# One core, attention with memory beside a gated feed-forward: fewer matmuls, packed score tiles, and transposes taken off the matmul engine

## The chip, the cores and the metric

The kernel runs on one core of one Trainium2 chip. The metric is device time in microseconds (us). Lower is better. A time given for a kernel is the median of its runs. The span is the time from the first to the last instruction of the one run that was profiled.

Five engines matter here. PE does matrix multiplies, DVE elementwise work and 32x32 transposes, ACT exponentials and other functions, and POOL the causal mask. SP only issues DMA transfers. ACT can issue them as well; its issues are called ACTq in the trace, those of SP are called SPq.

## The reference

The input x has 2048 tokens and 512 channels. The output is a per-token mix of two branches that read the same x.

```python
g = sigmoid((x * gate_w).sum(-1, keepdims=True))
out = g * A(x) + (1 - g) * B(x)

def B(x):                       # 512 -> 1792 -> 512
    gate, up = x @ W_gate, x @ W_up
    return (gate * (gate > 0) * up) @ W_down

def A(x):                       # 32 heads of 16 channels, 4 segments of 512 tokens
    q, k, v = x @ wq, x @ wk, x @ wv
    for s in range(4):
        a_dot = softmax(q_s k_s^T / 4 + causal_mask) @ v_s
        a_mem = phi(q_s) @ M / (phi(q_s) @ z + 1e-6)      # phi(t) = t+1 if t>0 else exp(t)
        o_s   = sigmoid(beta) * a_mem + (1 - sigmoid(beta)) * a_dot
        M, z  = M + phi(k_s)^T v_s, z + sum(phi(k_s))
    return concat(o) @ wo
```

## The kernel before

The program is a list of tasks for each engine. A scheduler written in Python runs when the kernel is built. It estimates when each task could start, chooses the order on each engine, and inserts semaphore waits. On the chip every engine then follows its list in order. The products of large weights with x ("weight matmuls" below: Q, K, V, gate, up, down, output) fill the time between the attention tasks.

A score tile has keys on the partitions and queries along the columns. Block `j` of 128 keys is seen only by queries from `128*j` on, so it has 512, 384, 256 or 128 columns. Four heads are computed at once, on four strips of 32 rows of the array. A head has only 16 channels, so K is projected with padded weights `wkp`: pairs of heads go to two padded copies.

```python
# K twice: padded (8 x 4 matmuls of 512 columns a segment), then with tokens on partitions (4 x 4)
for n in range(8):
    ... pe.matmul(A(ep)[:, :], lhsT=wkp[:, kt, n, :], rhs=xT[:, kt, tok0:tok0 + 512], ...)      # L622
for tt in range(TT):                      # not in the last segment
    ... pe.matmul(A(ep)[:, :], lhsT=xT[:, kt, ...128 tokens...], rhs=wk[:, kt, :], ...)         # L642

# scores and exp: one group and one exp for each key block j
for n in range(8):                        # 4 segments x 8 x 4 = 128 groups
    for j in range(4):
        N = 512 - 128 * j
        for jj in range(4):
            ... pe.matmul(PL[:, jj, 0:N], lhsT=kp16[32*jj:32*jj+32, s2, n, 128*j:128*j+128],
                          rhs=qT16[32*jj:32*jj+32, s2, G, 128*j:512], tile_position=(32*jj, 0)) # L771
        act.activation(E[:, e, :, 0:N], PL[:, :, 0:N], Exp, scale=SCALE)                        # L777
        pool.affine_select(E[:, e, :, 0:128], ...)        # causal mask of the diagonal block   # L779

# value product, then turned to tokens-on-partitions by PE
... pe.matmul(A(epv)[32*jj:32*jj+17, 128*j:512], lhsT=vaug[:, s2_, j, h, :], rhs=E[...])        # L722
dve.tensor_copy(pvT[:, r, :], A(epv)[:, :])
for i in range(4):
    pe.transpose(Tm[:, i*128:(i+1)*128], pvT[:, r, i*128:(i+1)*128], ident)                     # L738
... divide by the row sum into adot; adot = adot * gexp + amem;
    pe.transpose of adot into oT (L834), copied by DVE
# ... the feed-forward: DVE does both max(gate, 0) and the product with up                       # L812, L813

# start: one DMA queue, SP, in this order
wk, wq, x chunk 0, wv, gate column, beta, wg, wu, x chunks 1-3, wo, wd     # 4 transposed pieces a chunk
```

`PL` is the one score buffer. It holds four banks of 512 columns, so scores and exp alternate strictly. `A(ep)` is one of four accumulator banks. All of this is cut.

The softmax here doesn't subtract the row's maximum and nothing guards it: scores larger than these inputs give would overflow.

## Time and profile before

| | before |
|---|---|
| device time | 347.67 us (3 runs, 347.4 to 349.05) |
| span in the profile | 346.7 us |
| PE / DVE / ACT busy | 318.3 / 251.4 / 180.5 us |
| weight matmuls | 1040 |
| score groups, exps | 128, 128 |
| PE transposes | 192 |

The lines below are from the profile page: busy time of each engine (share of the span), then the busy share in 40 equal slices in tenths (9 is 90% or more), the granted PE clock in tenths of full speed, then the shares of the chain of waits that ended last, and the group of the exps (count, busy us and mean ns, idle time before them and what ended it).

```profile
span 346.7 us, 6188 instructions
PE 318.3 (92%) x2560; PEld 132.7 (38%) x2560; DVE 251.4 (73%) x560; ACT 180.5 (52%) x165; POOL 91.4 (26%) x141
...
PE   0995899999999999999989889999898999999996
...
PEclk9999699999999999999999999999999999999999
...
PE 74%; DVE 14%; SPq 9%; issue 1%; DMA 1%; ACT 0%; DVEq 0%
...
L777 ACT ACTIVATE E<-psL 128x2048 bf16<-128x2048 f32 (+3 forms) x128 | 158.2, 1236 | 108.5 <-PE psL L771 108.3
```

PE bounds this kernel: it is busy in nearly every slice and is most of the chain. Three slices differ: the first, with no work, the fourth, half full, and the fifth, with a lower clock. The timeline of PE shows them. Its columns are start, length, engine, line, operation, tiles, count, and in brackets the idle time before with what ended it.

```profile
8.86 6.50 PE L609 MATMUL psA<-xT,wq 128*128 128x512 bf16 x16 [8.86 <-DVE wkp L547]
...
35.91 1.84 PE L581 MATMUL psA<-gwc,xT 128*128 128x1 bf16 x64 [5.37 <-DMA xT<-in_A_x_dram]
...
38.42 3.62 PE L642 MATMUL psA<-wk,xT 128*128 128x512 bf16 x8
41.84 1.99 PE L609 MATMUL psA<-xT,wq 128*128 128x512 bf16 x8
```

Nothing runs for 8.86 us. At 30 us PE stands for 5.37 us, because the tiny gate product (one column) needs all of x and PE works in order. After both pauses the clock is half for a while: eight K matmuls need 3.62 us at 38.42, eight Q matmuls 1.99 us at 41.84.

Between those, the same timeline shows what single steps cost. These are four PE transposes, four weight matmuls, four more, and a score group of 128 columns.

```profile
157.00 0.40 PE L738 MATMUL psA<-ident,pvT 128*128 128x128 bf16 x4
157.23 1.03 PE L609 MATMUL psA<-xT,wq 128*128 128x512 bf16 x4
158.10 1.03 PE L801 MATMUL psA<-xT,wg 128*128 128x512 bf16 x4
159.06 0.23 PE L771 MATMUL psL<-qT,kp 32*128 32x128 bf16 x4
```

Lengths overlap, because a matmul's end lies after the start of the next. The time something costs PE is the step from its start to the next start. Four weight matmuls cost 158.10 - 157.23 = 0.87 us (about 216 ns each) and four transposes 0.23 us.

Summed over the whole trace in this way (each matmul counted until the next one starts or it ends itself, whichever comes first; this is my own working from the trace's times), the 318.3 us of PE are 243.6 us of weight matmuls, 32.0 of scores, 20.8 of value products, 12.5 of transposes and 9.4 of memory and gate products. The rest of the span is idle: 8.9 us at the start, 16.4 in between and 3.1 at the end. Of the 16.4 us, 5.4 are the wait for x above. The groups of instructions put 2.9 us to the transposes at L834, which wait for DVE's last combination, 2.7 us to weight matmuls that wait for an accumulator which DVE's memory reads (L682) still hold, and 3.4 us to scores that wait for an exp.

Entering a score group or value product from a weight matmul costs PE something too. The last weight matmul before one takes 312 or 309 ns to the next start instead of 216. There are 120 such places in this trace, which makes 11.6 us; a transpose after a weight matmul adds next to nothing of this kind.

### The profile page before, as it was taken

What the parts mean: (1) busy time and instruction counts of PE and PEld (TensorE: products, weight loads), DVE (VectorE), ACT (ScalarE), POOL (GpSimd) and SP (SyncE); (2) the same over time, 40 slices, a digit from 0 to 9 for tenths busy, and PEclk for the clock granted to TensorE, in tenths of its full rate; (3) what the DMA queues carried; (4) which work ended last, traced back from release to release, by engine and by line L of the source; (5) the groups of instructions that cost most, each with busy time, mean ns of one, the idle gap of its engine ahead of it and who ended that gap; (6) DMA issues with size and microseconds to landing.
All of it is one profiled execution on the core that took longest, in us unless ns stands there. A gap on an engine that the chain in (4) does not pass through costs nothing.

```text
span 346.7 us, 6188 instructions
## 1 busy us (share of the span) xinstructions
PE 318.3 (92%) x2560; PEld 132.7 (38%) x2560; DVE 251.4 (73%) x560; ACT 180.5 (52%) x165; POOL 91.4 (26%) x141
## 2 busy tenths in 40 slices
PE   0995899999999999999989889999898999999996
PEld 0331443434444444444443334433433334444442
DVE  7685399999998642699899896337988843679621
ACT  1566476566675555577654665555555555450000
POOL 8021023222224222222232232222332222220000
PEclk9999699999999999999999999999999999999999
DMA  7795440000000000000000000000000000000000
GB/s 183 258 306 94 139 145 2 0 3 3 0 3 2 0 17 30 17 0 3 2 0 2 0 2 0 32 16 17 0 2 0 2 15 32 16 2 0 2 30 31
DMA packets 16699, 12.19 MB, mean 35 GB/s; under 512 B 9760, under 2 KB 15648, under 8 KB 16672
## 3 DMA queue, kind: packets, MB, share of 16 engines
q1 hardware_dynamic: 16672, 11.81, 11.8%
q8 instruction: 20, 0.33, 0.4%
q14 instruction: 7, 0.06, 0.1%
HBM read 7.61 MB, written 2.10 MB: 28 GB/s over the span
## 4 chain that ended last, share of the span: by engine, by line
PE 74%; DVE 14%; SPq 9%; issue 1%; DMA 1%; ACT 0%; DVEq 0%
PE psA L857 14%; PE psA L806 13%; PE psA L801 12%; SPq L503 8%; PE psL L771 7%; PE psA L722 5%; PE psA L622 5%; PE psA L849 4%; PE psA L642 3%; PE psA L609 3%; DVE adot L824 3%; PE psA L631 3%; PE psA L738 3%; DVE amem L682 2%; DVE hT L813 2%
## 5 line engine op out<-in xcount | busy, mean ns | idle before, releaser
L777 ACT ACTIVATE E<-psL 128x2048 bf16<-128x2048 f32 (+3 forms) x128 | 158.2, 1236 | 108.5 <-PE psL L771 108.3
L779 POOL TENSOR_SCALAR_AFFINE_SELECT E<-E 128x512 bf16<-128x512 bf16 x128 | 83.9, 655 | 219.6 <-ACT E L777 219.6
L806 PE MATMUL psA<-xT,wu 128*128 128x512 bf16 x224 | 57.8, 380 | 1.6 <-DVE amem L682 1.3
L801 PE MATMUL psA<-xT,wg 128*128 128x512 bf16 x224 | 57.7, 380 | 0.9 <-DVE amem L682 0.8
L857 PE MATMUL psA<-wd,hT 128*128 128x512 bf16 x224 | 53.1, 380 | 0.8 <-DVE hT L813 0.8
L813 DVE TENSOR_TENSOR hT<-psA,rl 128x512 bf16<-128x512 f32 x56 | 38.5, 688 | 9.7 <-PE psA L806 8.6
L812 DVE TENSOR_SCALAR rl<-psA 128x512 bf16<-128x512 f32 x56 | 38.4, 686 | 7.1 <-PE psA L801 6.4
L771 PE MATMUL psL<-qT,kp 32*128 32x256 bf16 (+3 forms) x512 | 40.4, 305 | 3.4 <-ACT E L777 3.4
L861 DVE SCALAR_TENSOR_TENSOR osb<-psA,omg_all,zero 128x512 bf16<-128x512 f32 x16 | 12.0, 751 | 35.7 <-PE psA L857 34.4
L771 PEld LDWEIGHTS psL<-qT,kp 32*128 32x128 bf16 x512 | 12.9, 91 | 54.5 <-issue 27.1
L622 PE MATMUL psA<-xT,wkp 128*128 128x512 bf16 x128 | 31.0, 380 | 0.9 <-DVE amem L682 0.6
L857 PEld LDWEIGHTS psA<-wd,hT 128*128 128x128 bf16 x224 | 20.5, 98 | 24.8 <-issue 1.6
L732 DVE CAST pvT<-psA 128x512 bf16<-128x512 f32 x32 | 22.0, 689 | 10.4 <-PE psA L722 10.0
L801 PEld LDWEIGHTS psA<-xT,wg 128*128 128x128 bf16 x224 | 19.7, 98 | 24.9 <-DVE amem L682 2.3
L806 PEld LDWEIGHTS psA<-xT,wu 128*128 128x128 bf16 x224 | 18.9, 98 | 23.4 <-DVE amem L682 2.1
L609 PE MATMUL psA<-xT,wq 128*128 128x512 bf16 x64 | 18.3, 435 | 8.9 <-DVE wkp L547 8.9
L625 DVE CAST kp<-psA 128x512 bf16<-128x512 f32 x32 | 21.9, 686 | 5.0 <-PE psA L622 4.8
L722 PE MATMUL psA<-E,vaug 128*17 128x256 bf16 (+3 forms) x512 | 23.1, 300 | 0.2 <-DVE hT L813 0.2
L682 DVE SCALAR_TENSOR_TENSOR amem<-psA,gexp,ndrec 128x128 bf16<-128x128 f32 x48 | 16.4, 342 | 0.7
L849 PE MATMUL psA<-wo,oT 128*128 128x512 bf16 x64 | 16.5, 380 | 0.1
L743 DVE RECIPROCAL rden<-psA 128x16 f32<-128x16 bf16 x32 | 8.0, 250 | 11.6 <-PE psA L738 11.6
L622 PEld LDWEIGHTS psA<-xT,wkp 128*128 128x128 bf16 x128 | 11.1, 98 | 13.5 <-issue 0.9
(65 smaller groups left out, 260.3 us busy)
## 6 DMA issues: line engine op xcount, KB each, us to landing
out_dram<-osb SPq DMA_DIRECT2D x16, 128.0 KB
wg<-in_B_W_gate_dram SPq DMA_DIRECT2D x1, 1792.0 KB
wu<-in_B_W_up_dram SPq DMA_DIRECT2D x1, 1792.0 KB
wd<-in_B_W_down_dram SPq DMA_DIRECT2D x1, 1792.0 KB
wk<-in_A_wk_dram SPq DMA_DIRECT2D x1, 512.0 KB
wq<-in_A_wq_dram SPq DMA_DIRECT2D x1, 512.0 KB
wv<-in_A_wv_dram SPq DMA_DIRECT2D x1, 512.0 KB
wo<-in_A_wo_dram SPq DMA_DIRECT2D x8, 64.0 KB
```

The lines of the kernel that those rows point to most:

```text
L609: ins = pe.matmul(A(ep)[:, :], lhsT=wq[:, kt, G * 128:(G + 1) * 128], rhs=xT[:, kt, tok0:tok0 + 512], start=(kt == 0), stop=(kt == KT - 1))
L622: ins = pe.matmul(A(ep)[:, :], lhsT=wkp[:, kt, n, :], rhs=xT[:, kt, tok0:tok0 + 512], start=(kt == 0), stop=(kt == KT - 1))
L722: ins = pe.matmul(A(epv)[32 * jj:32 * jj + 17, 128 * j:512], lhsT=vaug[:, s2_, j, h, :], rhs=E[:, es[j], jj, 0:N], start=(j == 0), stop=(j ...
L771: ins = pe.matmul(PL[:, jj, 0:N], lhsT=kp16[32 * jj:32 * jj + 32, s2, n, 128 * j:128 * j + 128], rhs=qT16[32 * jj:32 * jj + 32, s2, G, 128 ...
L777: act_t.append(Tk("act", lambda ac, e=e, N=N: ac.activation(E[:, e, :, 0:N], PL[:, :, 0:N], ACT.Exp, scale=SCALE), reads=[f"bankL{q4}" for ...
L779: pool_t.append(Tk("pool", lambda pl, e=e: pl.affine_select(out=E[:, e, :, 0:128], in_=E[:, e, :, 0:128], compare_op=ALU.is_ge, fill=0.0, ...
L801: ins = pe.matmul(A(ep)[:, :], lhsT=wg[:, kt, f * 128:(f + 1) * 128], rhs=xT[:, kt, tok0:tok0 + 512], start=(kt == 0), stop=(kt == KT - 1))
L806: ins = pe.matmul(A(ep)[:, :], lhsT=wu[:, kt, f * 128:(f + 1) * 128], rhs=xT[:, kt, tok0:tok0 + 512], start=(kt == 0), stop=(kt == KT - 1))
L812: dve_t.append(Tk("dve", lambda dv, ep=epg, r=r: dv.tensor_scalar(rl[:, r, :], A(ep)[:, :], 0.0, None, ALU.max), writes=[f"rl{r}"], dur=c_ ...
L813: dve_t.append(Tk("dve", lambda dv, ep=epu, r=r, f=f: dv.tensor_tensor(hT[:, f, :], A(ep)[:, :], rl[:, r, :], ALU.mult), reads=[f"rl{r}"], ...
L849: ins = pe.matmul(A(ep)[:, :], lhsT=oT[:, G, i * 128:(i + 1) * 128], rhs=wo[:, G, :], start=(G == 0), stop=False)
L857: ins = pe.matmul(A(ep)[:, :], lhsT=hT[:, f, i * 128:(i + 1) * 128], rhs=wd[:, f, :], start=False, stop=(f == NF - 1))
```

## The change

The intent is to take work off PE, which bounds, and put some of it on engines with time left.

- **One K projection.** K is projected once, without padding. DVE writes two masked copies in place of the padded heads. The token-major copy for the memory comes from a DMA transpose of `ek`. PE does 928 weight matmuls in place of 1040.
- **Packed score tiles.** Blocks of 384+128 and 256+256 columns share a full tile of 512. There are 80 groups and 80 exps of one shape, in place of 128 of four shapes. The columns are the same in all.
- **No PE transposes.** DVE transposes the value product by 32x32 blocks, twice. The memory's result is turned by DMA. 192 PE transposes disappear.
- **A new scheduler.** It may also place the feed-forward's ReLU and the last scaling on ACT or on DVE.
- **A new start.** All weights are issued by ACT and x by SP, both from the first moment, and twelve dummy matmuls warm up PE.

The diff is very long, since the file is nearly rewritten. This is its core; cuts are marked with `...`.

```diff
 # start
-    all loads queued on "sp": wk, wq, x0, wv, gate, beta, wg, wu, x1..x3, wo, wd
+    def wload(name, dst, src, nbytes):
+        loads.append(dma("act", lambda e: e.dma_start(dst, src), nbytes, ...))
+    ... wq, wk, gate column, beta, wv, wg0, wu0, wg1, wu1, wo, wd
+    xl = [dma("sp", ... e.dma_start_transpose(V.xT[:, kt, c*512:(c+1)*512], A_x[...])) ...]
+    def f_warm(e):
+        for i in range(12):
+            e.matmul(PL[:, 0, :], lhsT=V.rl[:, 0, 0:128], rhs=V.rl[:, 0, :], start=True, stop=True)
 # K
-    for n in range(8): ... matmul(lhsT=wkp[:, kt, n, :], rhs=xT...)        # padded
-    for tt in range(TT): ... matmul(lhsT=xT..., rhs=wk[:, kt, :])           # token-major
+    ep = pj(V.wk, G, "k", "wk")                                             # 4 projections, once
+    dve.tensor_copy(V.kT[:, G, :], A(ep)[:, :])
+    for p in range(2):
+        dve.tensor_scalar(V.kp[:, ks, :], V.kT[:, G, :], V.pm[:, p:p+1], None, mult)   # L538, mask
+    ... phi into V.ek; sp.dma_start_transpose(V.phik[...], V.ek[:, G, :])
 # scores
-    for j in range(4): group of 512 - 128*j columns, exp of the same width
+    eA[0] = quad(f"{G}A0", [(n0, 0, 0, 512)])
+    eB[0] = quad(f"{G}B0", [(n0, 1, 0, 384), (n0, 3, 384, 128)])
+    flush()                                       # value products of the pair of heads before
+    eC = quad(f"{G}C", [(n0, 2, 0, 256), (n1, 2, 256, 256)])
+    ... A1, B1 for n1
+    act.activation(V.E[:, e, :, :], PL[:, :, :], Exp, scale=SCALE)          # L620, always 4 x 512
 # after the value product
-    dve.tensor_copy(pvT, A(epv)); pe.transpose x4; ... pe.transpose of adot; dve copies
+    dve.transpose(V.Tn[:, p, :], A(ep)[:, :])                               # L645
+    ... scale by the row sum and the gate in the transposed layout
+    dve.transpose(V.oTt[:, :], V.adT[:, :])                                 # L657
+    dve.tensor_tensor(V.oT[:, os_, :], V.oTt, V.amemT[:, G, :], add)        # amemT: DMA transpose
 # feed-forward: one operation, two possible engines
-    dve.tensor_scalar(rl, A(ep), 0.0, None, max)
+    Op([("act", ... activation(V.rl[:, r, :], A(ep)[:, :], Relu)), ("dve", ... tensor_scalar(... max))])
 # queues of PE, by priority
+    sc.queue(0, Q["patt"])     # scores and value products in ONE strict order
+    sc.queue(1, Q["pmu"]); sc.queue(1, Q["pnd"]); sc.queue(2, Q["pproj"]); sc.queue(3, Q["pout"]); sc.queue(4, Q["pffn"])
```

## The prediction

> **What bounds it now.** Engine table: PE busy 318.3 of 346.7 us (92%), DVE 251.4 (73%), ACT 180.5 (52%). PE is 74% of the chain of waits. PE's 28 us idle, by the groups and waits views: 8.9 us before the first Q matmul, 5.4 us for the last x chunks at 30 to 36 us, about 3 at the end, the rest small stalls. The window table shows a granted clock of 0.62 at 35 to 44 us after that stall; the first 16 Q matmuls run at a 430 ns pitch (timeline) against 216 later. The Trainium skill, "TensorE: Matmul & The Clock Gate" (Part 1), says that the array runs at half rate until about 3.4 us of activity and again after an idle window; the trace agrees both times. Together they cost about 7 us.
>
> **PE work, costed by the timeline's start-to-start times.**
> - 512-column weight matmuls: 1040 to 928, since one K projection (64) replaces a padded (128) and a token-major one (48). At 216 ns: minus 24 us.
> - Score matmuls: same columns, but 80 groups of 512 columns replace 128 groups of 512, 384, 256 and 128. A group costs its columns plus about 0.2 us of entering and leaving: 44 us to 35, minus 9.
> - PE transposes (128+64, about 0.23 us per four) go: minus 11 to 12.
> - Value matmuls, memory update and read: about minus 2.
> Sum: 309 us of full-clock work to about 264. All of it is on the critical path, since PE bounds.
>
> **Other engines (estimates from before's durations).** Exp: 128 instructions, 158 us, become 80 of 1.88 us, 150; with phi, 25 ReLUs and 10 final scalings ACT reaches about 190. DVE loses evictions, 25 ReLUs and chains of small memory operations; it gains 48 transposes of 512 columns (taken as 0.69 us, like its other PSUM reads; the Trainium skill, "VectorE: DVE Perf Modes" (The three transpose paths), has them as 32x32 blocks only, which suits this layout; no run here shows one yet) and 32 masks of 0.29 us. About 208 us, 72% of the new span. Neither becomes the bound. The score/exp loop needs about 80 x 2.6 = 210 us, under PE. DMA transposes for keys and memory should hide inside a segment.
>
> **Start.** Warm-up matmuls should remove most of the 3.5 us of half-rate Q. x transposes now go out on SP from the start, weights on ACT. Before, transposes queued behind the big weights held SP for 4.9 and 5.2 us; now they only share the engines. I expect first Q at 8 to 10 us, and a wait of 2 to 6 us for x chunks around 20 to 32. Danger: ACT issues 6 MB or more of weights before its first activation; if these issues are held likewise, the tiny exp of beta is late, DVE sits behind it in order, PE runs out of accumulators, and up to 10 us are lost.
>
> **Time.** 264 work + 9 start + 3 end + 4 x wait + 2 residual half clock + 8 small stalls = 290 us. Range 278 to 304.
>
> **What would show it right.** 928 weight matmuls at 216 ns; PE busy 265 to 280 including warm-up; score groups about 35 us; 80 exps at 1.88 us; PSUM transposes near 0.69; the chain mostly PE; PE idle about 25 us, mostly at the start; no second half-clock slice, or a short one.
>
> **What would make it wrong.** DVE transposes much slower than 0.69 us, PE waiting for accumulators (above 304). DMA transposes landing several us late, so that memory matmuls, in order on PE, stall each segment. ACT held at the start. Packed score groups have two pieces, which may cost more than I read. On the low side: stalls almost gone, 275 to 280.

## The result, and the profile after

| | before | after |
|---|---|---|
| device time | 347.83 us (4 runs) | 295.57 us (4 runs, 295.05 to 296.37) |
| ratio, 95% interval | | 0.8491, 0.8468 to 0.8513 |
| span in the profile | 346.7 | 293.3 |
| PE busy | 318.3 | 269.9 |
| first Q matmul starts at | 8.9 us | 17.8 us |

A ratio is the mean time of one kernel's fast runs over the mean time of the other's fast runs of the same rounds. It is therefore not quite the ratio of the medians quoted. The result is correct, as are those of all experiments below.

The same lines of the page, for the kernel after:

```profile
span 293.3 us, 5236 instructions
PE 269.9 (92%) x2136; PEld 115.0 (39%) x2172; DVE 198.7 (68%) x391; ACT 184.2 (63%) x142; POOL 93.4 (32%) x150
...
PE   7059989799999999999999999999999999999895
...
PEclk9658979999999999999999999999999999999999
...
PE 85%; DVE 6%; DMA 4%; issue 2%; SPq 1%; ACT 0%; DVEq 0%; ACTq 0%
```

PE still bounds. It is busy from the ninth slice on, and hardly at all in the second, where "before" was at work. The busy share is 92% both times, and yet 53 us are gone: a share alone says nothing of the amount of work.

These lines are the timeline of all engines at the start, in the kernel after.

```profile
0.80 34.50 SPq L437 DMA_TRANSPOSE xT<-in_A_x_dram  x16
1.25 5.30 PE L468 MATMUL psL<-rl 128*128 128x512 bf16 x12 [1.25 <-DVE rl L460]
...
10.17 5.88 ACTq L412 DMA_DIRECT2D wo<-in_A_wo_dram  x1
16.08 2.81 ACTq L412 DMA_DIRECT2D wd<-in_B_W_down_dram  x1
...
17.81 1.87 PE L522 MATMUL psA<-xT,wq 128*128 128x512 bf16 x4 [11.26 <-DMA xT<-in_A_x_dram]
...
20.21 0.23 ACT L472 ACTIVATE eb<-braw 128x32 f32<-128x32 bf16 x1
21.18 1.91 PE L522 MATMUL psA<-xT,wq 128*128 128x512 bf16 x4
...
24.16 1.03 PE L522 MATMUL psA<-xT,wq 128*128 128x512 bf16 x4
```

The warm-up ends at 6.55 us. Then PE stands for 11.26 us until a piece of x lands. The first Q matmuls run at half clock all the same (four in 1.91 us at 21.18; 1.03 at 24.16). ACT's issues of `wo` and `wd` are held for 5.88 and 2.81 us, so its first small exponential comes only at 20.21 us.

The costs of the new operations are in the groups of instructions by shape (count, then busy us and mean ns).

```profile
L620 ACT ACTIVATE E<-psL 128x2048 bf16<-128x2048 f32 x80 | 150.1, 1876 | 44.3 <-PE psL L615 43.8
...
L645 DVE STREAM_TRANSPOSE Tn<-psA 128x512 f32<-128x512 f32 x32 | 21.5, 698 | 17.6 <-PE psA L640 17.4
...
L657 DVE STREAM_TRANSPOSE oTt<-adT 128x512 bf16<-128x512 bf16 x12 | 8.4, 703 | 0.1
```

Next come the same start-to-start sums as before, in us. One correction was needed. The trace of "after" has 2136 matmul records but all 2172 records of weight loads (PEld, one for each matmul). The missing ones are weight matmuls, and without the correction they look like idle time. Where a gap before a weight matmul has one load more than matmuls, I put a matmul back, 216 ns before the next one. That restores 31 of 36 in "after", 46 of 46 in e9 and 31 of 35 in e5; the last few would move about 1 us from idle to weight matmuls. "before" misses none.

The third column is experiment e9 below (the old work under the new scheduler and with a good start), the fourth e5 (the new kernel with a good start).

| | before | after | e9 | e5 |
|---|---|---|---|---|
| span | 346.7 | 293.3 | 328.1 | 281.6 |
| weight matmuls | 243.6 | 212.4 | 239.2 | 210.3 |
| of it, added by half clock | 4.6 | 4.4 | 1.4 | 1.6 |
| scores | 32.0 | 26.4 | 31.8 | 26.4 |
| value products | 20.8 | 19.9 | 21.0 | 19.7 |
| PE transposes | 12.5 | 0 | 12.0 | 0 |
| memory, gate | 9.4 | 9.4 | 9.7 | 9.4 |
| warm-up | 0 | 5.3 | 4.7 | 4.7 |
| idle before the first weight matmul | 8.9 | 12.5 | 4.3 | 4.0 |
| other idle in between | 16.4 | 3.9 | 2.0 | 4.2 |
| end | 3.1 | 3.3 | 3.2 | 2.9 |
| entries from weight matmuls to scores or value products | 120 | 77 | 122 | 78 |

### The profile page after: what moved, and what is told of

Read it like the earlier page. It is cut to its first block, busy times and chain, and to the rows that moved or that the text cites. A ratio compares the mean times of both kernels' runs of the same rounds, so it can differ in the third digit from the quotient of the medians.

```text
span 293.3 us, 5236 instructions
## 1 busy us (share of the span) xinstructions
PE 269.9 (92%) x2136; PEld 115.0 (39%) x2172; DVE 198.7 (68%) x391; ACT 184.2 (63%) x142; POOL 93.4 (32%) x150
## 4 chain that ended last, share of the span: by engine, by line
PE 85%; DVE 6%; DMA 4%; issue 2%; SPq 1%; ACT 0%; DVEq 0%; ACTq 0%
PE psA L685 32%; PE psA L716 17%; PE psA L522 10%; PE psL L615 8%; PE psA L640 6%; PE psA L708 5%; DMA xT<-in_A_x_dram 4%; PE psA L520 4%; SPq L437 1%; DVE vaug L546 1%; DVE kp L538 1%; PE psA L561 1%; PE psA L590 1%; DVE gexpT L494 1%; DVE qT L529 1%
## 5 line engine op out<-in xcount | busy, mean ns | idle before, releaser
L620 ACT ACTIVATE E<-psL 128x2048 bf16<-128x2048 f32 x80 | 150.1, 1876 | 44.3 <-PE psL L615 43.8
L645 DVE STREAM_TRANSPOSE Tn<-psA 128x512 f32<-128x512 f32 x32 | 21.5, 698 | 17.6 <-PE psA L640 17.4
L615 PE MATMUL psL<-qT,kp 32*128 32x384 bf16 (+3 forms) x512 | 31.7, 301 | 0.9 <-ACT E L620 0.8
L522 PE MATMUL psA<-xT,wq 128*128 128x512 bf16 x58 | 18.1, 432 | 11.8 <-DMA xT<-in_A_x_dram 11.3
L693 ACT ACTIVATE rl<-psA 128x512 bf16<-128x512 f32 x25 | 14.9, 596 | 16.8 <-PE psA L685 16.8
L529 DVE CAST qT<-psA 128x512 bf16<-128x512 f32 x16 | 11.0, 688 | 19.4 <-PE psA L522 19.3
L694 DVE TENSOR_SCALAR rl<-psA 128x512 bf16<-128x512 f32 x31 | 21.1, 682 | 4.1 <-PE psA L685 3.6
L640 PE MATMUL psA<-E,vaug 128*17 128x256 bf16 (+3 forms) x512 | 21.1, 300 | 0.0
L522 PE MATMUL psA<-xT,wk 128*128 128x512 bf16 x62 | 18.6, 418 | 0.3 <-issue 0.2
L721 ACT ACTIVATE osb<-psA,omg 128x512 bf16<-128x512 f32 x10 | 6.9, 687 | 17.3 <-PE psA L716 17.3
L520 PE MATMUL psA<-wv,xT 128*128 128x512 bf16 x61 | 15.0, 380 | 0.3 <-issue 0.2
L640 PEld LDWEIGHTS psA<-E,vaug 128*17 128x17 bf16 x512 | 10.5, 90 | 11.2 <-issue 4.2
## 6 DMA issues: line engine op xcount, KB each, us to landing
wg<-in_B_W_gate_dram ACTq DMA_DIRECT2D x2, 896.0 KB, 14.1
```

The costliest lines, as they stand in the source:

```text
L520: ins = e.matmul(A(ep)[:, :], lhsT=V.xT[:, kt, tok + col * 128:tok + (col + 1) * 128], rhs=w[:, kt, :], start=(kt == 0), stop=(kt == KT - 1))
L522: ins = e.matmul(A(ep)[:, :], lhsT=w[:, kt, col * 128:(col + 1) * 128], rhs=V.xT[:, kt, tok:tok + 512], start=(kt == 0), stop=(kt == KT - 1))
L615: ins = q.matmul(PL[:, jj, o:o + w], lhsT=V.kp[32 * jj:32 * jj + 32, kslot(s, n), 128 * j:128 * j + 128], rhs=V.qT[32 * jj:32 * jj + 32, q ...
L620: acts.append(act(lambda a, e=e: a.activation(V.E[:, e, :, :], PL[:, :, :], ACT.Exp, scale=SCALE), t_act(2048), reads=[f"bankL{b}" for b i ...
L640: ins = q.matmul(A(ep)[32 * jj:32 * jj + 17, c:512], lhsT=V.vaug[:, s % 2, j, 8 * G + 2 * jj + p, :], rhs=V.E[:, e, jj, o:o + w], start=(j ...
L645: ds.append(dve(lambda e, p=p, ep=eps[p]: e.transpose(V.Tn[:, p, :], A(ep)[:, :]), t_dve(512), writes=[f"Tn{p}"], name=f"tr{s}_{G}_{p}", e ...
```

## The experiments

The theory from here on: the three parts that take work off PE are worth what their PE time says, about 45 us together, and the new start loses some 10 us of it. The rivals: the gain comes from the scheduler or from the relief of DVE, or the parts are worth something else than their PE time. Twelve kernels were run in three sets (e1 to e4, e5 to e8, e9 to e12); kernels of one set share the runs of "before" (347.8, 348.41 and 348.47 us in the three sets). "After" was run in a set of its own, so a difference to it of less than about 1 us says nothing.

| run | what it is | us | ratio to before | 95% |
|---|---|---|---|---|
| after | the change | 295.57 | 0.8491 | 0.8468 to 0.8513 |
| e1 | after, old K projections | 323.32 | 0.9283 | 0.9247 to 0.9318 |
| e2 | after, scores not packed | 326.35 | 0.9382 | 0.9354 to 0.9411 |
| e3 | after, PE transposes | 323.19 | 0.9303 | 0.9268 to 0.9339 |
| e4 | after, all three undone | 365.53 | 1.0511 | 1.0478 to 1.0544 |
| e5 | after, other start | 283.23 | 0.8114 | 0.8069 to 0.8159 |
| e6 | after, PE's attention queue split | 301.84 | 0.8637 | 0.8597 to 0.8678 |
| e7 | e6, scores not packed | 326.09 | 0.9348 | 0.9299 to 0.9398 |
| e8 | e6, PE transposes | 311.89 | 0.8927 | 0.8881 to 0.8972 |
| e9 | all three undone, queue split, other start | 330.50 | 0.9482 | 0.9442 to 0.9521 |
| e10 | after, no work moved to ACT | 299.20 | 0.8577 | 0.8543 to 0.8612 |
| e11 | e5 without warm-up | 283.04 | 0.8116 | 0.8092 to 0.8140 |
| e12 | e5, longer warm-up, gate copies on ACT and DVE | 282.19 | 0.8088 | 0.8064 to 0.8112 |

### e1: K projected twice again

```diff
-            ep = pj(V.wk, G, "k", "wk")                  # then DVE masks into two copies
+            for p in range(2):
+                ep = pj(V.wkp, 2 * G + p, "k", "wkp")    # padded weights, straight to kp
+        for G in range(4 if s < NSEG - 1 else 0):
+            ep = pj(V.wk, G, "kt", "wk", True)           # token-major, no DMA transpose
```

The padded weights need space, so `hT` has 19 slots instead of 20.

> The changed kernel with its single K projection undone: zero-padded K weights (128 matmuls) plus a token-major K projection (48) in place of 64, no masks and no DMA transposes of the key features; one hidden-layer buffer slot fewer (19 of 20) for room. Theory P (PE is full, so its arithmetic is the time): 112 more matmuls at 0.216 us = 24 us, 318 to 323 us, PE busy about 294. Rival S (the gain came from the new scheduler filling holes, and extra PE work would be hidden in part): under 312. Rival D (DVE load is what mattered): DVE gains about 6 us of evictions net, so 300 to 305.

It took 323.32 us, 27.7 more than "after". 112 matmuls of 216 ns are 24.2 us. PE's busy time on the page rose from 269.9 to 293.9 us, which is 24.0. The rest includes a stall of 2.75 us at 20 us into the run. The time is 0.3 us over the expected range. The part is worth its arithmetic, to within a few us.

### e2: scores not packed

```diff
-            pes.append(pe(fq, ...)); acts.append(act(... E[:, e, :, :] <- PL[:, :, :] ...))
+            for pt in parts:                              # each part its own group and exp
+                o, w = pt[2], pt[3]
+                pes.append(pe(lambda q, pt=pt: fq(q, (pt,)), ...))
+                acts.append(act(... V.E[:, e, :, o:o + w] <- PL[:, :, o:o + w] ...))
```

> The changed kernel with its score tiles unpacked: each piece of 512, 384, 256 and 128 columns is again its own group with its own exp (128 instead of 80), same buffers otherwise. Theory P: 48 more entries and exits of row-tiled groups at about 0.2 to 0.27 us, 305 to 309 us; exp goes from 150 to about 158 us of ACT. Rival S: hidden, 296 to 300. A second rival, that the score/exp loop itself bounds: each of the 48 extra round trips costs 0.5 us or more, over 318.

It took 326.35 us, 31 more. PE's work grew by 14 us (scores 33.7 us instead of 26.4; weight matmuls and value products 6.7 us more, half clock included). The other part is idle time in between, 20.3 us instead of 3.9: PE is at half clock and partly idle from 280 to 307 us. So the arithmetic of 9 us does not explain this run: theory P failed by 17 us, the time is where the second rival had put it (over 318), and e7 was made to find out why.

### e3: PE transposes

```diff
-                e.transpose(V.Tn[:, p, :], A(ep)[:, :])                # DVE
+                e.tensor_copy(V.pvT[:, p, :], A(ep)[:, :])             # DVE
+                q.transpose(A(ep)[...bitcast bf16...], V.pvT[:, p, ...], V.ident)   # PE, x4
...
-            amemT by DMA; e.transpose(V.oTt, V.adT); add
+            adot = adot * gexp + amem; q.transpose(... V.adot ...); e.tensor_copy(V.oT, ...)
```

> The changed kernel with attention output turned by PE again: DVE evicts to bf16, PE transposes 128 + 64 tiles, normalisation token-major, memory term added token-major, no DVE transposes and no DMA transposes of the memory term. DVE time stays about equal. Theory P: PE +12.5 us of transposes plus some entering and leaving: 307 to 311 us. Rival S: hidden in idle PE, 296 to 301. If DMA transposes of the memory term were costing waits in the changed kernel, the result lies lower than P says, 303 to 306.

It took 323.19 us, 27.6 more and 12 above theory P's range, for 14.3 us of transposes. Here too the clock is half near the end, from 284.6 to 305 us, and the idle time in between is 15.8 us. The transposes stood in the one strict queue with the scores. e8 tests that.

### e4: all three undone

This is e1, e2 and e3 together (`hT` 18 slots), with the start of "after".

> All three undone together on the new scheduler, with the changed kernel's start and its choice of ACT or DVE for ReLU and final scaling (hidden-layer slots 18 for room). Theory P: the parts add up, 295.6 + 24 + 11 + 13 = about 341 to 347 us; what is left to the kernel before (347.8) is the scheduler, the ACT/DVE choice and the start together, 1 to 7 us. Rival S: the scheduler is worth 15 us or more, so 320 to 332.

It took 365.53 us, more than "before" and 18.5 above the expected range. The three parts cost 70 us in this form, not 45. The first weight matmul started at 17.4 us, and the idle time in between was 22.3 us. The old work in the new frame, start and queue order included, is worse than the old work in the old frame. e9 separates the start and the queue from the rest.

### e5: another start

```diff
-        loads.append(dma("act", ...))
+        loads.append(dma("act" if name in ("wq", "wk", "braw") else "sp", ...))
-    sc.queue(0, loads)
-    sc.queue(0, xl)
+    sc.queue(0, [w["wq"], w["wk"], w["braw"]])
+    sc.queue(0, xl[0:4] + [w["wv"], w["gw"]] + xl[4:8] + [w["wg0"], w["wu0"]] + xl[8:16]
+                + [w["wg1"], w["wu1"], w["wo"], w["wd"]])
```

The same bytes move, but ACT issues only what the first matmuls need. Everything else stands in one queue with x, in the order in which it is needed.

> The changed kernel with the order of loads alone altered: x chunks, V weights, gate column and the large weights go out on SP in one queue in the order of first use; ACT issues only the Q and K weights and beta. Theory C (in the changed kernel the first x chunk lands at 17.6 us because 6 MB of weights share the DMA engines with it): first Q matmul at 8 to 10 us, half-clock stretch gone or short, 284 to 288 us. Rival T (transposes issued on SP are slow by themselves, or the ACT queue was not what held them): first Q still after 15 us, 293 to 297. If later x chunks now come too late, a stall of a few us appears at 20 to 40 us and the gain shrinks to 3 to 5.

It took 283.23 us, 12.3 less than "after" and 0.8 below the expected range. The timeline of PE at the start of e5:

```profile
1.25 4.73 PE L469 MATMUL psL<-rl 128*128 128x512 bf16 x12 [1.25 <-DVE rl L461]
8.69 1.86 PE L523 MATMUL psA<-xT,wq 128*128 128x512 bf16 x4 [2.70 <-DMA xT<-in_A_x_dram]
```

The first Q matmul starts at 8.69 us instead of 17.81, and the half clock lasts for 7 full steps of about 427 ns instead of 12 (a shorter first step, and in "after" a shorter last one, come on top). The reason stands in the view of DMA issues. Its last number is the median time from issue to landing, in us. First "after":

```profile
xT<-in_A_x_dram SPq DMA_TRANSPOSE x16, 10.2
```

and then e5:

```profile
xT<-in_A_x_dram SPq DMA_TRANSPOSE x16, 3.9
```

In "after", the pieces of x shared the way with weights that ACT had issued at the same time and that nobody needed yet. The landing records in the trace show it: the fourth piece, issued at 4.70 us, landed at 17.62 in "after", later than `wv` (13.82) and half of `wg` (16.70); in e5 it was issued at 4.69 and landed at 8.45. The Trainium skill, "DMA: Bandwidth & Descriptors" (Issuing engines are not separate DMA queues), says that DMAs started by different engines "will ultimately run on the same 16 DMA engines and interleave with each other". The runs agree: a second issuing queue gave no second path, and it gave up the order. e5 changes the queue and the order together; the same order on two queues was not run. In e5 the same SP queue issued, one after the other, as its timeline shows (start, length):

```profile
0.80 5.15 SPq L436 DMA_TRANSPOSE xT<-in_A_x_dram  x4
6.00 0.58 SPq L412 DMA_DIRECT2D wv<-in_A_wv_dram  x1
```

The fall of 12.3 us is larger than the 9.1 us by which the first Q moves. The sums above give the rest: half clock adds 2.8 us less (4.4 to 1.6). So the start of "after" costs about 12 us, shown by exchanging it alone.

### e6: PE's attention queue split

```diff
-    sc.queue(0, Q["patt"])
+    for pr, px in ((0, "quad"), (0, "ptr"), (1, "pv"), (1, "otr")):
+        sc.queue(pr, [t for t in Q["patt"] if t.name.startswith(px)])
```

Score groups no longer wait in the list behind value products. This is the control for e7 and e8.

> Control for the next two: the changed kernel with score groups and value matmuls in two scheduler queues, as the kernel before had them, in place of one strict queue. Nothing else. Expected within 1.5% of 295.6 us either way; a larger move would mean that queue order matters by itself.

It took 301.84 us, 6.3 more than "after" and 2.1% where at most 1.5% was expected. The trace says where. In "after", 5 value products follow a weight matmul directly; the others follow a score group, as the strict list has them. In e6 it is 27, at about 95 ns each, which is 2.1 us. The value products themselves take 21.1 us instead of 19.9. The gate product waits 2.2 us instead of 0.7, and the first Q starts 0.7 us later. So the strict order is worth some 3 us in the changed kernel (2.1 and 1.2), and 2.2 us lie in the start. Those 2.2 us follow the landing of x: its last piece lands at 39.18 us in e6 and at 38.09 in "after", and among the kernels with this start the first Q varies from 17.2 to 18.8 us. That the queue edit caused them is not shown. Half clock adds 1.5 us less in e6, so about 2.5 us more are spread over small terms that were not traced.

### e7: scores not packed, queue split

This is e6 with the edit of e2.

> Unpacked score tiles as in the second experiment (326.4 us, with 14 us of waits in the score/exp loop at its end, after the weight matmuls had run out), but with score groups and value matmuls in two queues. Theory L (the loop of score, exp, score has become the bound: about 0.9 us per round trip beyond the exp, 128 trips instead of 80): still 318 us or more, the last exp later than 285 us, PE idle at the end. Rival H (the strict queue held score groups behind value matmuls): the tail goes, 304 to 309 us.

It took 326.09 us, as long as e2 (326.35), and 24.3 more than its control e6. So the strict queue is not the reason why unpacking costs more than its arithmetic; the rival H falls. The timeline of PE in e7 near the end shows the reason, theory L of the text:

```profile
283.42 0.51 PE L615 MATMUL psL<-qT,kp 32*128 32x512 bf16 x4 [0.70 <-ACT E L622]
284.12 1.24 PE L642 MATMUL psA<-E,vaug 128*17 128x512 bf16 x16 [0.19 <-POOL E L625]
285.91 0.51 PE L615 MATMUL psL<-qT,kp 32*128 32x384 bf16 x4 [0.54 <-ACT E L622]
```

No weight matmuls are left from 280 to 299 us; PE waits for each exp, since there is one score buffer. The loop of scores and exp runs from 32.1 to 297.6 us in e7, which is 265.5 us for 128 trips or 2.07 us each. In "after" it runs from 31.6 to 261.6, which is 230 us for 80 trips or 2.88 us each. Packing therefore shortens two things: PE's work, and a second loop beside it that must not last longer than PE's other work. The 2.07 us are no floor of the loop: with nothing in between, from 283.42 to 292.03, five trips take 1.72 us each. Whether another order, with fewer weight matmuls between the early trips, would have avoided the tail was not tried. The windows view of e7 gives, for 26 us of this stretch, the busy time of the engines and the granted clock:

```profile
core 0: us, PE busy (x) PEld busy (x) DVE busy (x) ACT busy (x) POOL busy (x), PEclk, DMA share, GB/s
275.00:301.00 26.00, 12.72 (x128) 4.15 (x127) 7.97 (x14) 16.32 (x15) 8.25 (x13) 0.66 0.00 1
```

PE is busy for 12.72 of 26 us at a clock of 0.66.

### e8: PE transposes, queue split

This is e6 with the edit of e3.

> PE transposes put back as in the third experiment (323.2 us, where the strict queue made every score group stand behind a transpose that waits for its eviction), now with the transposes and score groups in queues of their own as in the kernel before. Theory P (PE arithmetic is the time): 307 to 311 us, little idle at the end. Rival W (the round trip PE, DVE, PE of a PE transpose lengthens the attention chain whatever the queues): still 318 us or more with a tail of waits.

It took 311.89 us, 11.3 less than e3 and 10.05 more than its control e6. The transposes are 11.7 us of PE in it. There is no tail at half clock: the loop ends at 258.0 us. Theory P holds (its range was missed by about 1 us), and W falls: in e3 the score groups had stood in the strict queue behind transposes that waited for DVE. Against its control the part costs a little less than its PE time; the first Q comes 1.3 us earlier in e8 than in e6.

### e9: the old work in the new frame

K twice, unpacked scores and PE transposes, with the split queue and the start of e5 (`wk` loaded first, `hT` 18 slots).

> The work of the kernel before (padded and token-major K, 128 score groups, PE transposes) on the new scheduler, now with the score groups, value matmuls and transposes in queues of their own and with the start of the fifth experiment (first Q near 9 us). The strict version with the slow start took 365.5 us, the kernel before takes 348. Theory R (the 18 us of difference are the start, 12 us as the fifth experiment measured, and the strict queue's transposes): 340 to 349 us, so scheduler and ACT/DVE choice by themselves are worth nearly nothing for that work. Rival S (the new scheduler is worse for that work, since its score/exp loop outlasts the weight matmuls): over 352, with PE idle and at half clock near the end. Rival B (the new scheduler is better): under 338.

It took 330.5 us: 18 less than "before" with the same weight, score, value and transposing matmuls, and 47 more than e5. Theory R (340 to 349) failed, and the time is in the range of rival B: for this work the new program is better. Its loop also has 128 trips and lasts 264 us, from 14.1 to 278.4 us. The windows view, with the same columns, shows its last 50 us, when the loop is over:

```profile
278.00:328.00 50.00, 45.58 (x235) 20.95 (x238) 15.85 (x27) 12.31 (x20) 0.64 (x1) 1.00 0.05 17
```

Here weight matmuls are left over when the loop ends, and the clock stays at 1.00. That is why the same loop costs nothing in e9 and much in e7: PE has 319 us of work in e9, and 290 in e7.

The step from e9 to e5 is the three parts under equal conditions, except for the queue split (e6). The table of sums splits the 46.5 us of span. The 112 matmuls are 24.2 us, the transposes 12.0 us, the scores themselves 5.4 us and the value products 1.3 us. A further 3.9 us come from fewer entries (78 places instead of 122, each measured by its excess over 216 ns: 7.85 us instead of 11.7). That is 46.8, and the prediction had 45. Not all of it need be the parts: e6 shows 1.2 us of value products for the queue split alone, as much as the 1.3 here, and of the 44 entries fewer, 8 are entries to value products (4 instead of 12), which the strict list also saves.

The step from "before" to e9 is 18.6 us of span with the same 1040 weight matmuls. It is not PE work: 14.4 us of it are idle time in between (16.4 to 2.0), and 3.2 us are half clock. Of the idle time 5.4 us are the wait for x; the other 9 are small waits of PE for DVE and ACT that the new program no longer has. Three things are new in e9 that could do this: the scheduler, the choice between ACT and DVE, and a shorter memory read on DVE. They were not separated, so the cause of these 9 us stays open. (e10 below takes the choice away from the changed kernel, and its small waits after the start do not come back; for the old work this was not run.) It is not a lower cost of entries; their number is the same, 120 and 122.

e4 differs from e9 by 35 us. The first weight matmul is 8.3 us later in e4, and its idle time in between is 22.3 us instead of 2.0. Of that idle time 17.5 us lie after 311 us, because the loop ends only at 331.1 us; in e9 it ends at 278.4. How much of this is the strict queue and how much the late start was not separated.

### e10: no work moved to ACT

```diff
-    Op([("act", ... Relu ...), ("dve", ... max ...)])
+    Op([("dve", ... max ...)])               # the last scaling likewise
```

> The changed kernel with all ReLUs and all final scalings on DVE, as in the kernel before, in place of a choice between ACT and DVE. DVE busy goes from 199 to about 222 us, ACT from 184 to 163. Theory P (DVE has slack, PE is the time): 294 to 299 us. Rival D (relief of DVE is a large part of the gain): 302 or more.

It took 299.2 us, 3.6 more than "after" and just outside the expected range. DVE is busy for 219.5 us instead of 198.7, ACT for 164.6 instead of 184.2. But PE's timeline shows where the time is: first Q 1.0 us later, a wait of 5.00 us before the gate product at 33 us, where "after" has 0.70, and half clock until 45.3 us. These are the gate product in e10 and then in "after":

```profile
38.32 1.85 PE L486 MATMUL psA<-gwc,xT 128*128 128x1 bf16 x64 [5.00 <-DVE ttmp L541]
```

```profile
38.63 1.74 PE L486 MATMUL psA<-gwc,xT 128*128 128x1 bf16 x64 [0.70 <-DVE kp L538]
```

The view names DVE, but the wait is one for x. The last piece of x lands at 37.86 us in e10 and at 38.09 in "after" (landing records of the trace). In all seven kernels with this start whose PE stood here (after, e2, e3, e6, e7, e8, e10), the gate product starts 0.46 or 0.55 us after that landing. In "after", PE's list held enough other work before the gate product; in e10's list it ran out 4.6 us earlier.

After 45.3 us PE is as full as in "after". So DVE at 73% does not hold up PE in the steady part. The relief of DVE as a cause of the gain is not supported; what this run shows is another order of PE's list at the start.

### e11: no warm-up

e5 without the twelve dummy matmuls.

> The fifth experiment (283.2 us) without the twelve warm-up matmuls. There they were followed by 2.7 us of idle and a half-clock stretch of 3.4 us was left. If the warm-up saves half-clock time, this is 1.5 to 2.5 us slower (half clock for two stretches of 3.4 us in place of one), 284.5 to 286; if the idle time undoes it, the same within 0.5 us.

It took 283.04 us against e5's 283.23: the second of the two outcomes expected, the same within 0.5 us. The first Q matmul starts at 8.69 us in both, and the half-clock stretch is 5 full steps in e11 against 7 in e5. A warm-up that ends 2.7 us before the work begins is worth nothing here. The Trainium skill, "TensorE: Matmul & The Clock Gate" (Part 1, What's actually happening), says that the array is at half rate by default, that a busy window of about 3.4 us frees it, and that this window runs freely, so that the number of slow matmuls changes with its phase. That fits 5 and 7, and a single trace of each does not tell more.

### e12: the fastest version

```diff
-        for i in range(12):                  # e5's warm-up
+        for i in range(24):
...
-            gd.append(dve(lambda e, ...: e.tensor_copy(V.gexpT[...], V.gexp[...])))
+            gd.append(Op([("act", ... ACT.Copy), ("dve", ... tensor_copy)]))   # became 12 DVE, 4 ACT
```

> The fifth experiment (283.2 us) with 24 warm-up matmuls in place of 12, so that PE is busy until the first x chunk is in, and 4 of the 16 small gate copies on ACT in place of DVE (the scheduler may choose; DVE spent 3.9 us on them in a row and PE then waited 1.8 us). Half-clock stretch at the first Q gone: minus 1.7 us; gate copies: minus 0.5 to 1. Expected 280.3 to 282.5 us, the fastest of all.

It took 282.19 us (281.78 to 282.3), the fastest of all, 0.85 us under e11 on the same chip with no overlap of their ranges. The timeline of PE at its start:

```profile
1.25 6.74 PE L469 MATMUL psL<-rl 128*128 128x512 bf16 x24 [1.25 <-DVE rl L461]
8.64 1.02 PE L525 MATMUL psA<-xT,wq 128*128 128x512 bf16 x4 [0.65 <-DMA xT<-in_A_x_dram]
```

The warm-up reaches to 0.65 us before the first Q, and four Q matmuls take 1.02 us at once; in e5 they took 1.86. The stall of PE for the gate's copies (1.8 us at 48.9 us in e5) is gone; in its place PE waits 1.0 us at 44.9 us for an exp that stood behind gate copies on ACT. The two edits were not run apart.

## Why the prediction was right

The total was right: 290 predicted, 295.57 measured, in the range of 278 to 304. The PE work, nine tenths of the sum, was right term by term; that the total came so close is partly luck, since an error of 8.8 us at the start was offset by 8.1 us in two other terms. The terms of its sum against the span of 293.3 us:

| term | predicted | measured |
|---|---|---|
| full-clock PE work | 264 | 263.8 |
| start, to the first Q | 9 | 17.8 |
| wait for x | 4 | 0.7 |
| residual half clock | 2 | 4.4 |
| small stalls | 8 | 3.2 |
| end | 3 | 3.3 |

The measured 263.8 is the sum of PE's work in the table of sums (273.5 with the restored records) less the warm-up (5.3) and less what half clock added (4.4); the records that could not be put back would add up to 1 us to it and take as much from the stalls. The device time is 2.3 us above the profile's span.

**The step that failed** is this one: "I expect first Q at 8 to 10 us". It was 17.8. The sentence before it says that the transposes of x "now they only share the engines". They do, and this sharing is the cost: a median of 10.2 us from issue to landing, against 3.9 when the same bytes stand in one queue in order. e5 shows it, by 12.3 us. Had this step been known, the same sum would have given 299.

**What made up for it.** The wait for the later x pieces, taken as 4 us, was 0.7: with the start so late, PE still had other work until 37.93 us, and the last piece of x landed at 38.09. This was luck of the order; with the same start it was 2.2 us in e6 and 5.0 in e10. And the small stalls were 3.2 us instead of 8. The prediction carried most of the old program's small waits over; e9 against "before" shows that the new program does not have them.

**The three savings.** "Minus 24", "minus 9" and "minus 11 to 12" were 24.2, 9.3 (5.4 + 3.9) and 12.0 between e9 and e5. "About minus 2" for the rest was 1.3 in the value products, and the queue split alone may account for that (e6). Nearly all of it showed in the span (46.8 us of terms, 46.5 us of span), as predicted. The method held: counts times start-to-start steps read from the timeline, plus what each entry costs.

**Undoing one part alone** costs 27.7, 31 and 27.6 us, which is 86 together, where the three together are 47 (e9 against e5). Against their control e6, scores and transposes cost 24.3 and 10.05 (e7, e8). Such numbers do not add up, and they are not the worth of the parts. In e2 the score and exp loop outlasts PE's other work (shown by e7 and e9); in e3 the queue order adds to it (shown by e8).

**Other engines.** Exps of 1.88 us were right (80 of 1876 ns). Transposes of 0.69 us were right: 698 ns from PSUM. The masks were taken as 0.29 us and took 417 ns on average. DVE was predicted at 208 us and is 198.7; ACT at about 190 and is 184.2. None bounds. The score and exp loop was taken as 210 us and is 230; still below PE's work, but with less room than thought.

**Half clock.** The text put both pauses of "before" at about 7 us together, but this sum had in it the time that PE would have needed anyway. Counted by step, 22 matmuls at up to 427 ns instead of 216 add 4.6 us in "before", and 21 in "after" add 4.4. The prediction also gave about 3.4 us of activity as what ends the half rate; each of the two stretches of "before" lasted 5.9 us. The warm-up removed nothing in "after", since an idle time of 11.26 us followed it. The Trainium skill, "TensorE: Matmul & The Clock Gate" (Part 1), gives 426.7 and 215.7 ns for the two states at 512 columns. The traces agree.

**The danger that was named**, ACT held by its issues, came about (5.88 us for one issue; the exp of beta at 20.21 us), but it was hidden behind the longer wait for x. It cost nothing that could be seen in this trace.

## What to carry to other kernels

Cost a change on the bounding engine by counts times start-to-start steps, but cost the start apart: list what the first matmul needs, and load that first, in one queue in order of need; here bulk weights on a second queue did not come for free, they delayed it (median landing of x 10.2 us against 3.9). When you test a part by undoing it, undo it in a frame that suits it, or compare against a control with the same frame: a second loop that outlasted the filler work turned 9 us into 31 here (24 against the control). And check the count of records before you read a gap as idle time. A warm-up that ended 2.7 us before the real work was worth nothing here; with one that reached to 0.65 us before it, no half-clock step was left. And the engine that a view names beside a wait need not be the cause: compare the landing of the data.

## What the Trainium skill lacked or had wrong

- "DMA: Bandwidth & Descriptors" (Issuing engines are not separate DMA queues) says that issuing on several engines only saves the sequencer's time. It lacks the harm: bulk weights issued by ACT brought the median landing of x pieces on SP from 3.9 to 10.2 us, and the whole kernel 12.3 us (e5 against "after").
- "Perfetto Trace Analysis" (DMA Instruction — HWDGE) has a lock wait inside the profiled time of an issue, but no page that was found gives a size for an issue that is held. ACT's issues took up to 5.88 us in "after" (2.65, 1.90, 5.88 and 2.81 us among the later ones), where the first two took 0.43 and 0.53. Whether it is this wait was not shown.
- "VectorE: DVE Perf Modes" (The three transpose paths) gives one size, 128x128 bf16 at 311 ns. A reader needs the wide ones: 128x512 took 698 ns as f32 from PSUM, and 703 ns as bf16 from SBUF to SBUF, so bf16 from SBUF was no faster than f32 from PSUM.
- "TensorE: Matmul & The Clock Gate" (Part 1) puts the penalty of warming up at under 1% of a typical span. The first stretch alone is close to that, 2.9 of 346.7 us in "before" and 2.9 of 293.3 in "after" (0.8 and 1.0%); with the second stretch, after a pause, it was 1.3 and 1.5%. Its warning that a trace's clock events are not reliable holds: the clock record of "before" shows 1.00 in the first Q stretch, where the steps are at half rate.
